# Attention and a gated MLP on one core: small tiles placed elsewhere in SBUF

## The chip, the cores and the metric

The kernel runs on one core of a Trainium2 chip. The metric is the device time of one launch in microseconds (us). The kernel before takes 735.44 us, the median of three runs (735.39 to 735.93). Its profile is of one further execution, which took 734.27 us and has a span of 732.5 us.

## The reference

Inputs are x (8 batches, 8 heads, 512 tokens, 64 wide) and state (the same with 32 tokens), float32. Cut to what matters:

```python
scores  = x @ state.T / 8 ;  a  = softmax(scores)  ; xread = a  @ state
scores2 = state @ x.T / 8 ;  a2 = softmax(scores2) ; sread = a2 @ x
y   = concat([xread, sread], axis=2)      # per batch 544 rows, heads joined to 512 columns
out = ((y @ w_a) * (y @ w_b)) @ w_out     # 512 -> 1536 -> 512
```

## The kernel before, in words

All heavy work is matrix products on TensorE. Each large product has 128 rows of contraction, 128 stationary columns (the weights) and 512 moving columns of 4 bytes, that is 2,048 bytes in each of the 128 SBUF partitions. Numbers are split into a high and a low part (type fp32r), so one product of the mathematics is three instructions: high by high, high by low, low by high.

The program has these kinds of product:

- **Layer 1** (output tile `ab`, function `layer1`): `(y @ w_a)` and `(y @ w_b)` for one of 12 strips of 128 hidden columns. Weights: slices of `p_h`, `p_l`. Moving: `at_h`, `at_l` (the attention weights of a batch; the state and the weights were multiplied beforehand into `p_h`, `p_l`). A strip is 2 x 2 x 3 = 12 instructions of 512 columns.
- **Layer 2** (output tile `acc`, function `layer2`): the gated strip times `w_out`. Weights: slices of `g_h`, `g_l`. Moving: the two halves of `wo0` ... `wo11`, of 2,048 bytes each. A strip is 4 blocks of tokens x 3 = 12 instructions of 512 columns.
- **Projections** (output tile `ms`, early `acc`, function `project`): the states times `w_a` and `w_b`. Weights: `sd_h`, `sd_l`. Moving: `wq`.
- **States** (output tile `ab`, class `States`): layer 1 for the rows of sread, 256 moving columns. Weights: `wq` and `sw_st`. Moving: `x_nat` and `x_raw`. Its layer 2 is as above.
- The attention's own products in full float32 (output `ms`), few and short.

ScalarE (ACT) and VectorE (DVE) move results out of PSUM, split them in two parts and convert the 64-bit weights; transfers are issued from SyncE (SP). The code records all instructions, and a planner (`plan`) then fixes one order for every engine from its own cost and due-time figures; all instructions of the program are issued from line 1047, which is why the profile's rows bear that line, and are told apart by their tiles.

**Where tiles stand in SBUF.** Pools are laid out one after the other in the order in which they are opened, each pool's tiles in turn, each with as many buffers as asked for. Below the first pool lie 16,512 bytes of each partition (32 x 512 + 128). Nearly all tiles have a multiple of 512 bytes a partition. Two do not: `m1` (3 x 16 numbers, 192 bytes, two buffers, 384 bytes in all) and `m2` (4 numbers, 8 buffers of 32 bytes, 256 bytes in all), both small tiles of the softmax in the pool `att`. So a tile's start past a multiple of 512 bytes depends on which of the two lie ahead of it. PSUM tiles are whole banks and are the same before and after.

Of the kernel before, what the change touches and what calls it, by code (L numbers as in the profile page):

```python
# [10 lines left out]
F32 = mybir.dt.float32  # L11
# [9 lines left out]
P = 128  # L21
# [393 lines left out]
def attn_moe(ctx, tc, xt, xn, sd, wl, w_out, out):  # L415
# [9 lines left out]
    def pool(name, bufs, free=False, **kw):  # L425
        p = Pool(ctx.enter_context(tc.tile_pool(name=name, bufs=bufs, **kw)), name, bufs, free)
        pools.append(p)
        return p

    const0 = ctx.enter_context(tc.tile_pool(name="const0", bufs=1))  # L430
    const = pool("const", 1)
    proj = pool("proj", 2)
    att = pool("att", 2)
    mlp = pool("mlp", 2)
    dram = pool("dram", 1, space=bass.MemoryType.DRAM)
    ps_acc = pool("ps_acc", 4, space=bass.MemoryType.PSUM)
# [6 lines left out]
    def minus(eng, out, in0, in1):  # L443
        eng.tensor_tensor(out=out, in0=in0, in1=in1, op=ALU.subtract)
# [149 lines left out]
    class Attention:  # L594
# [37 lines left out]

        def soft_t(self):

            m1 = self.m1 = att.tile([P, 3, 16], F32, name="m1")
            sp = self.sp
            t = self.t.rearrange("p (a b) -> p a b", b=32)
            nc.vector.tensor_reduce(out=m1[:, 0, :], in_=t, axis=AX.X, op=ALU.max)
            minus(nc.vector, sp, t, m1[:, 0, :].unsqueeze(2).broadcast_to([P, 16, 32]))
# [9 lines left out]

        def soft(self):  # L650

            m2 = self.m2 = att.tile([P, 4], F32, name="m2", bufs=8)
            nc.vector.tensor_reduce(out=m2[:, 0:1], in_=self.s, axis=AX.X, op=ALU.max)
            nc.vector.tensor_scalar_mul(out=m2[:, 1:2], in0=m2[:, 0:1], scalar1=-SCALE)
            if self.b not in WIDE:
                self.turn()
            nc.scalar.activation(out=self.e2, in_=self.s, func=AF.Exp, bias=m2[:, 1:2], scale=SCALE,
                                 accum_out=m2[:, 2:3])

        def turn(self):  # L660
            sp = self.sp
            nc.vector.transpose(out=sp.rearrange("p a b -> p (a b)"), in_=self.s)

            m1 = self.m1 = att.tile([P, 3, 16], F32, name="m1")
            nc.vector.tensor_reduce(out=m1[:, 0, :], in_=sp, axis=AX.X, op=ALU.max)
            minus(nc.vector, sp, sp, m1[:, 0, :].unsqueeze(2).broadcast_to([P, 16, 32]))

# [422 lines left out]
```

## Time and profile before

| | |
|---|---|
| median of 3 runs | 735.44 us |
| profiled execution | 734.27 us, span 732.5 us |
| TensorE (PE) busy | 706.2 us, 96% of the span, 3,440 matmuls |
| weight loads (PEld) busy | 557.7 us, beside the matmuls |
| VectorE (DVE) busy | 495.8 us, 68% |
| ScalarE (ACT) busy | 394.9 us, 54% |
| DMA | 134.32 MB, mean 183 GB/s |

Matmuls are pipelined: a row's duration (about 0.39 us for 512 columns) reaches into the next one. What a matmul costs when TensorE is full is the distance from its start to the start of the next, so the starts are what to read.

### The profile page before, as it was taken

Reading aid. Unit: us, or ns where it says so; the run is one execution under the profiler, and the core shown is the slowest. Engines: PE = TensorE matmul, PEld = TensorE weight load, DVE = VectorE, ACT = ScalarE, POOL = GpSimd, SP = SyncE. Lnnn points to the kernel's source line nnn. Section 1 sums busy time; section 2 is a strip of 40 time slices with the busy share of each in tenths; the row PEclk is TensorE's granted clock in tenths of the full one; section 3 lists DMA queues with packets and bytes.
Section 4 is the critical chain, followed back from the end, with each engine's and each line's share of the span. In section 5 each row is a group of like instructions: output and inputs, shape, how many; then the busy total and the mean of one; then the engine's idle time right before and its main releaser. Section 6 shows DMA issues by size and latency. Waiting matters only on the chain.

```text
span 732.5 us, 9629 instructions
## 1 busy us (share of the span) xinstructions
PE 706.2 (96%) x3440; PEld 557.7 (76%) x3440; DVE 495.8 (68%) x947; ACT 394.9 (54%) x723; POOL 0.7 (0%) x6
## 2 busy tenths in 40 slices
PE   5898899998999999999999999999999999999997
PEld 4565657785887888788888887886788888988886
DVE  5986795995847967684799548637879833795322
ACT  4966785686846459786445325234456433553222
POOL 0000000000000000000000000000000000000000
PEclk9999999999999999999999999999999999999999
DMA  9667867677788436859988133324425311501002
GB/s 339 219 225 276 278 238 241 240 278 268 259 286 309 158 142 243 272 193 354 356 314 288 38 115 123 115 64 134 159 57 198 119 58 30 199 31 30 1 0 87
DMA packets 55087, 134.32 MB, mean 183 GB/s; under 512 B 5632, under 2 KB 5632, under 8 KB 55040
## 3 DMA queue, kind: packets, MB, share of 16 engines
q1 hardware_dynamic: 55040, 133.71, 52.5%
q8 instruction: 27, 0.44, 0.3%
q14 instruction: 20, 0.16, 0.1%
HBM read 87.03 MB, written 46.66 MB: 183 GB/s over the span
## 4 chain that ended last, share of the span: by engine, by line
PE 92%; ACT 5%; DMA 1%; DVE 1%; issue 1%; DVEq 0%; SPq 0%; ACTq 0%
PE ab L1047 40%; PE acc L1047 39%; PE ms L1047 13%; ACT wq L1047 2%; DMA p_raw<-scr 1%; DMA x_raw<-xt 0%; ACT stg L1047 0%; ACT t L1047 0%; ACT wo L1047 0%; ACT p_h L1047 0%; ACT sd_h L1047 0%; ACT e L1047 0%; DVE m L1047 0%; ACT sw_st L1047 0%; ACT at_h L1047 0%
## 5 line engine op out<-in xcount | busy, mean ns | idle before, releaser
L1047 PE MATMUL acc<-wo,g_h 128*128 128x512 f32 x816 | 259.3, 397 | 0.1
L1047 PEld LDWEIGHTS acc<-wo,g_h 128*128 128x128 f32 x816 | 151.4, 188 | 37.0 <-issue 2.3
L1047 DVE TENSOR_TENSOR a_sb<-ab,a_sb 128x512 f32<-128x512 f32 (+1 forms) x108 | 71.3, 661 | 138.9 <-PE ab L1047 131.8
L1047 PE MATMUL acc<-wo,g_l 128*128 128x512 f32 x408 | 159.3, 396 | 0.0
L1047 PE MATMUL ab<-at_h,p_h 128*128 128x512 f32 x384 | 152.4, 400 | 1.9 <-ACT p_h L1047 1.7
L1047 PE MATMUL ab<-at_l,p_h 128*128 128x512 f32 x384 | 152.2, 397 | 0.0
L1047 PE MATMUL ab<-at_h,p_l 128*128 128x512 f32 x384 | 150.8, 396 | 0.0
L1047 ACT COPY a_sb<-ab 128x512 f32<-128x512 f32 (+1 forms) x108 | 60.9, 564 | 150.7 <-PE ab L1047 149.6
L1047 ACT CAST g_h<-a_sb 128x512 fp32r<-128x512 f32 (+1 forms) x108 | 64.6, 598 | 53.2 <-DVE a_sb L1047 52.9
L1047 PEld LDWEIGHTS acc<-wo,g_l 128*128 128x128 f32 x408 | 76.5, 188 | 18.3 <-issue 1.0
L1047 PEld LDWEIGHTS ab<-at_h,p_h 128*128 128x128 f32 x384 | 73.0, 190 | 22.4 <-ACT p_h L1047 3.6
L1047 PEld LDWEIGHTS ab<-at_h,p_l 128*128 128x128 f32 x384 | 72.7, 189 | 20.1 <-issue 3.1
L1047 PEld LDWEIGHTS ab<-at_l,p_h 128*128 128x128 f32 x384 | 72.9, 190 | 17.0 <-issue 1.8
L1047 DVE TENSOR_TENSOR g_l<-a_sb,g_h 128x512 fp32r<-128x512 f32 (+1 forms) x108 | 70.8, 655 | 20.9 <-ACT g_h L1047 20.8
L1047 DVE TENSOR_TENSOR p_l<-p_raw,p_h 128x512 fp32r<-128x512 f32 x92 | 60.0, 684 | 11.7 <-ACT p_h L1047 11.7
L1047 ACT CAST p_h<-p_raw 128x512 fp32r<-128x512 f32 x92 | 52.8, 619 | 13.8 <-PE ab L1047 9.3
L1047 DVE TENSOR_SCALAR t<-t 128x512 int32<-128x512 int32 x120 | 49.8, 422 | 9.6 <-ACT t L1047 8.5
L1047 PE MATMUL ms<-wq,sd_h 128*128 128x512 f32 (+2 forms) x112 | 38.8, 418 | 7.3 <-ACT wo L1047 3.9
L1047 ACT CAST wq<-t 64x512 fp32r<-64x512 f32 (+1 forms) x64 | 39.4, 619 | 8.2 <-PE ms L1047 2.9
L1047 DVE SCALAR_TENSOR_TENSOR t<-raw,t 128x512 int32<-128x512 int32 (+1 forms) x60 | 39.7, 686 | 0.3
L1047 PE MATMUL ms<-wq,sd_l 128*128 128x512 f32 (+2 forms) x112 | 37.7, 406 | 0.0
L1047 ACT COPY wo<-ms 128x512 f32<-128x512 f32 x44 | 25.8, 590 | 12.8 <-PE ms L1047 11.5
(93 smaller groups left out, 702.2 us busy)
## 6 DMA issues: line engine op xcount, KB each, us to landing
p_raw<-scr SPq DMA_DIRECT2D x46, 512.0 KB, 4.4
scr<-sw_st SPq DMA_DIRECT2D x48, 256.0 KB, 4.2
scr<-wo SPq DMA_DIRECT2D x48, 256.0 KB, 4.2
raw<-wl SPq DMA_DIRECT2D x22, 512.0 KB, 5.8
part<-stg SPq DMA_DIRECT2D x20, 512.0 KB, 3.0
stg<-part SPq DMA_DIRECT2D x20, 512.0 KB, 6.1
out<-stg SPq DMA_DIRECT2D x34, 256.0 KB, 2.4
x_raw<-xt SPq DMA_DIRECT2D x14, 576.0 KB, 3.9
```

What stands on the lines that cost most here:

```text
L1047: getattr(obj, method)(*map(real, args), **{k: real(x) for k, x in kw.items()})
```

## The change

The two small tiles get pools of their own: `m1` stands in a new pool `small`, opened ahead of all others, and `m2` in a new pool `tail`, opened behind `att`. Numbers of buffers (2 and 8) and shapes stay. No instruction, wait, transfer or order of an engine differs; only addresses do.

```diff
+    small = pool("small", 2)
     const0 = ctx.enter_context(tc.tile_pool(name="const0", bufs=1))
     const = pool("const", 1)
     proj = pool("proj", 2)
     att = pool("att", 2)
+    tail = pool("tail", 8)
     mlp = pool("mlp", 2)
...
-            m1 = self.m1 = att.tile([P, 3, 16], F32, name="m1")
+            m1 = self.m1 = small.tile([P, 3, 16], F32, name="m1")
...
-            m2 = self.m2 = att.tile([P, 4], F32, name="m2", bufs=8)
+            m2 = self.m2 = tail.tile([P, 4], F32, name="m2")
...
-            m1 = self.m1 = att.tile([P, 3, 16], F32, name="m1")
+            m1 = self.m1 = small.tile([P, 3, 16], F32, name="m1")
```

With `m1` ahead, everything from `ident` to `x_raw` moves up by 384 bytes. What stood between `m1` and `m2` stays, what stood between `m2` and the end of `att` moves down by 256, and the pool `mlp` stays. In bytes past a multiple of 512:

| tiles | before | after |
|---|---|---|
| `ident`, `xst`, `raw`, `t1`, `t2`, `wq`, `sd_h`, `sd_l`, `sw_st`, `wo0` to `wo11`, `x_raw` | 128 | 0 |
| `s_p`, `x_nat`, `at_h`, `at_l` | 0 | 0 |
| `e2`, `a2`, `a_tr` | 256 | 0 |
| `stg`, `p_raw`, `p_h`, `p_l`, `a_sb`, `g_h`, `g_l` | 256 | 256 |

As slices of tiles begin at multiples of 512 bytes, this is by kind of product:

| product | moving start before | after | weights' start before | after |
|---|---|---|---|---|
| layer 1 (`ab`, 512 columns) | 0 | 0 | 256 | 256 |
| layer 2 (`acc`) | 128 | 0 | 256 | 256 |
| projections (`ms<-wq,sd`) | 128 | 0 | 128 | 0 |
| states (`ab`, 256 columns) | 0 (`x_nat`), 128 (`x_raw`) | 0 | 128 | 0 |

## Rows read from the trace of the kernel before

**Rows 1.** The page: busy time by engine; chain that ended last, by engine and line
```profile
PE 706.2 (96%) x3440; PEld 557.7 (76%) x3440; DVE 495.8 (68%) x947; ACT 394.9 (54%) x723; POOL 0.7 (0%) x6
...
PE 92%; ACT 5%; DMA 1%; DVE 1%; issue 1%; DVEq 0%; SPq 0%; ACTq 0%
PE ab L1047 40%; PE acc L1047 39%; PE ms L1047 13%; ACT wq L1047 2%; DMA p_raw<-scr 1%; DMA x_raw<-xt 0%; ACT stg L1047 0%; ACT t L1047 0%; ACT wo L1047 0%; ACT p_h L1047 0%; ACT sd_h L1047 0%; ACT e L1047 0%; DVE m L1047 0%; ACT sw_st L1047 0%; ACT at_h L1047 0%
```
**Rows 2.** Windows: length, busy time by engine, granted clock, DMA share, GB/s
```profile
98.00:176.00 78.00, 77.86 (x368) 59.78 (x368) 63.66 (x124) 51.66 (x95) 0.00 (x0) 1.00 0.74 257
176.00:186.00 10.00, 6.44 (x19) 3.90 (x18) 6.44 (x12) 9.46 (x17) 0.00 (x0) 0.83 0.77 262
186.00:728.00 542.00, 542.00 (x2611) 438.36 (x2610) 349.58 (x655) 263.98 (x484) 0.00 (x0) 1.00 0.46 157
```
**Rows 3.** Matmuls by tiles, 98 to 728.2 us: count, busy, mean ns, idle before
```profile
L1047 PE MATMUL acc<-wo,g_h 128*128 128x512 f32 x778 | 246.9, 396 | 0.0
L1047 PE MATMUL acc<-wo,g_l 128*128 128x512 f32 x390 | 152.4, 396 | 0.0
L1047 PE MATMUL ab<-at_h,p_h 128*128 128x512 f32 x360 | 142.3, 397 | 0.6 <-ACT p_h L1047 0.4
...
L1047 PE MATMUL ms<-wq,sd_h 128*128 128x512 f32 (+1 forms) x86 | 32.2, 419 | 3.1 <-ACT wo L1047 2.4 <-ACT sw_st L1047 0.8
...
L1047 PE MATMUL ab<-x_nat,wq 128*128 128x256 f32 x128 | 24.2, 281 | 0.0
```
**Rows 4.** The chain that ended last, pieces in time: start, length, what
```profile
349.13 2.73 PE ab L1047 x12
351.86 2.79 PE acc L1047 x12
354.66 2.73 PE ab L1047 x12
...
434.76 2.79 PE acc L1047 x12
```
**Rows 5.** Timeline of TensorE, 404 to 410 us: start, duration, instructions
```profile
404.23 0.39 PE L1047 MATMUL ab<-at_h,p_h 128*128 128x512 f32 x1
...
404.93 0.39 PE L1047 MATMUL ab<-at_h,p_h 128*128 128x512 f32 x1
...
406.97 0.62 PE L1047 MATMUL acc<-wo,g_h 128*128 128x512 f32 x2
...
409.76 0.39 PE L1047 MATMUL ab<-at_h,p_h 128*128 128x512 f32 x1
```
**Rows 6.** Timeline of all engines, end of the span, from 725.3 us
```profile
725.34 0.42 DVE L1047 TENSOR_TENSOR g_l<-a_sb,g_h 128x256 fp32r<-128x256 f32 x1 [0.47 <-ACT g_h L1047]
725.57 1.08 PE L1047 MATMUL acc<-wo,g_h 128*128 128x512 f32 x4
...
727.89 0.62 PE L1047 MATMUL acc<-wo,g_l 128*128 128x512 f32 x2
728.32 1.29 DVE L1047 TENSOR_TENSOR stg<-acc,stg 128x512 f32<-128x512 f32 x2 [2.55 <-PE acc L1047]
```
**Rows 7.** Timeline of TensorE: two projections, and a run of state products
```profile
101.37 0.39 PE L1047 MATMUL ms<-wq,sd_h 128*128 128x512 f32 x1
...
101.83 0.39 PE L1047 MATMUL ab<-at_l,p_h 128*128 128x512 f32 x1
...
720.66 0.28 PE L1047 MATMUL ab<-x_nat,sw_st 128*128 128x256 f32 x1
...
722.89 0.39 PE L1047 MATMUL acc<-wo,g_h 128*128 128x512 f32 x1
```
**Rows 8.** Timeline of TensorE around the one long stall behind 98 us
```profile
178.54 0.40 PE L1047 MATMUL ms<-wq,sd_l 128*128 128x512 f32 x1
181.30 0.50 PE L1047 MATMUL ms<-wq,sd_h 128*128 128x512 f32 x1 [2.36 <-ACT wo L1047]
...
183.96 0.63 PE L1047 MATMUL ab<-at_h,p_h 128*128 128x512 f32 x1
...
185.24 0.63 PE L1047 MATMUL ab<-at_h,p_h 128*128 128x512 f32 x1
```
**Rows 9.** Costliest groups by form: VectorE, tiles at 256, 128 and 0 bytes
```profile
L1047 DVE TENSOR_TENSOR g_l<-a_sb,g_h 128x512 fp32r<-128x512 f32 x96 | 65.7, 685 | 18.8 <-ACT g_h L1047 18.8
...
L1047 DVE SCALAR_TENSOR_TENSOR t<-raw,t 128x512 int32<-128x512 int32 x30 | 20.6, 686 | 0.2
...
L1047 DVE TENSOR_TENSOR s_p<-s_p,m 128x512 f32<-128x512 f32 x28 | 19.3, 690 | 0.8
```

## The prediction

> **What bounds the kernel now.** I read the page first, then windows, the chain of waits, and last the starts of single matmuls. The page's busy line and its chain [rows 1] show TensorE busy for 96% of the span and on the chain for 92% of it, layer 1 (`ab`) and layer 2 (`acc`) with 40% and 39%. The windows [rows 2] tell where that holds: from 98 to 176 us TensorE is busy for 77.86 of 78 us, from 186 to 728 us for all of 542 us, and only 176 to 186 us has a hole. In that whole stretch its idle time before matmuls of these kinds is 3.1 + 0.6 us, all of it behind ScalarE, none behind a transfer or VectorE [rows 3]. So behind 98 us a nanosecond saved per matmul is a nanosecond saved per matmul of the span; ahead of 98 us TensorE waits for others in many places, and I count nothing there.
>
> A busy TensorE is not one at its peak, so the next view is the chain in order of time [rows 4]. Between 349 and 437 us it is nothing but strips of 12 layer 1 matmuls and 12 layer 2 matmuls in turn. Both strips stream 12 x 512 columns with 12 weight loads, and yet layer 1 takes 2.73 us and layer 2 takes 2.79 us, each time. From the start at 351.86 to that at 434.76 there are 15 pairs: 82.90 / 15 = 5.527 us a pair.
>
> The timeline resolves this [rows 5]. Layer 2 goes from 406.97 to 409.76: 2.79 / 12 = 232.5 ns from start to start. Layer 1 has two speeds: its first three matmuls behind layer 2 go from 404.23 to 404.93, 0.70 / 3 = 233 ns, and the other nine from 404.93 to 406.97, 2.04 / 9 = 226.7 ns. [...]
>
> Is it other engines that disturb layer 2? At the end of the span no: VectorE's last work before the final results ends at 725.76 (725.34 + 0.42), and TensorE alone then takes 727.89 - 725.57 = 2.32 us for 10 layer 2 matmuls, the same 232 ns [rows 6].
>
> **The change part by part.** No instruction is added, removed or moved. What differs between layers 1 and 2 in the supply of operands is in the table of starts: the weights of both stand 256 bytes past a multiple of 512, the moving operand of layer 1 on the multiple, that of layer 2 128 bytes past it. A run of 2,048 bytes touches four pieces of 512 bytes from a multiple, and five from 128 past it. The change gives layer 2 the pair of starts that layer 1 has.
>
> *Layer 2.* 778 + 390 = 1,168 matmuls stand behind 98 us [rows 3]. If layer 2 runs as layer 1 does with its slow first three (2.735 us a strip, between the 2.73 of [rows 4] and the 2.74 of [rows 5]), each saves (2.79 - 2.735) / 12 = 4.6 ns: 5.4 us. If it runs as the nine do, 232.5 - 226.7 = 5.8 ns: 6.8 us. Bound on the other side: it stays, 0 us, or gets worse by as much as it could gain, -6.8 us, since no row shows this operand at another start. I take 5.4 us, the nearest row being layer 1's whole strip.
>
> *Layer 1.* Its first three matmuls behind layer 2 are slow with starts that are as good as those of the other nine, so they pay for what went before them. With layer 2 no longer different the cause would go: 0.70 - 3 x 0.2267 = 0.02 us by the rows; by the pair of 5.527 us, less 24 x 0.2267 = 5.440, less layer 2's 12 x 5.8 ns = 0.070, it is 0.017 us. Of 3 x 360 = 1,080 layer 1 matmuls behind 98 us [rows 3] make 90 strips: 1.5 us. Bounds 0 and 1.5; I take all of it, because the two layers then have equal starts.
>
> *Projections.* 2 x 86 = 172 matmuls. They now run at (101.83 - 101.37) / 2 = 230 ns [rows 7] with both operands 128 past; afterwards both are on the multiple, a pair that no row shows. Between the 226.7 ns of the best row and a loss as large, 3.3 ns x 172 = 0.6 us either way. I take 0.
>
> *States.* 128 + 64 + 64 + 32 = 288 matmuls of 256 columns, of which [rows 3] shows the first group. They take (722.89 - 720.66) / 19 = 117 ns [rows 7] with a moving start now of 0, now of 128, and weights at 128; afterwards 0 and 0. [...] I take 0.
>
> *VectorE, ScalarE, transfers.* The same kind of VectorE operation takes 685 ns with operands at 256, 690 at 0 and 686 at 128 [rows 9]: no effect of the start. Transfers to moved tiles may land sooner or later; TensorE waits for none behind 98 us [rows 3], so work of TensorE covers them. If that cover went, a late one would show as a new wait.
>
> *Who is late next.* In the hole at 176 to 186 us ScalarE is busy for 9.46 of 10 us [rows 2]; the stall of 2.36 us [rows 8] is ScalarE's. Its work there starts from a projection's result, so TensorE's gain ahead of it should pass on. If it does not, what layer 2 won before 176 us is lost: by the windows' counts (368 of 368 + 19 + 2,611 matmuls) 143 of the 1,168, x 4.6 ns, about 0.7 us. The lower clock behind the hole costs about 7 matmuls x 200 ns = 1.4 us (427 against 227); a shorter or longer hole could move this. I leave both in the range.
>
> Sum: 5.4 + 1.5 = 6.9 us off the profiled execution's 734.27 us, of which 732.5 are span. Its time lies 1.2 us below the median of 735.44, which I take as the base: 735.44 - 6.9 = 728.5 us.
>
> [...]
>
> **The rivals.**
> *The start is not what tells the layers apart.* Layer 2 also changes its moving half at each instruction and uses four PSUM banks in turn, where layer 1 stays in one for six matmuls. Then nothing changes: 735.4 us. For it: it needs no effect of addresses, which VectorE does not have either [rows 9]. Against: layer 1 changes its moving operand as well (`at_h`, `at_l`), and the slow three of layer 1 fall in the same bank as three fast ones [rows 5].
> [...]
> *Gains that do not pass on.* Layer 2 gets faster and ScalarE's hole, or VectorE elsewhere, takes back some: with half of 6.9 us kept, 732.0 us. Against: no idle time of TensorE from 186 to 728 us [rows 2].
>
> **How the numbers follow.** The forecast (728.5 us) 0.70; gains half kept (732.0) 0.11; nothing changes (735.4) 0.11; reads that meet (741.4) 0.08. A difference under 0.2%, about 1.5 us, can hardly be told from none with this kernel. The forecast's own range reaches from all gains together (6.8 + 1.5 + 0.6 + 1.0 = 9.9 us, 725.5) to layer 2 alone without the part before 176 us (5.4 - 0.7 = 4.7, 730.7). For 8 in 10 the range is taken up to the case without change: 725.5 to 735.5 us. Faster 0.81, same 0.11, slower 0.08.
>
> **What would show it.** Layer 2's strips in the chain at 2.73 us or below instead of 2.79 confirm the main term; layer 1's first three at 227 ns, and pairs of 5.44 to 5.47 us, the second. Strips that stay at 2.79 make it wrong, and point to the first rival. [...] A hole at 176 us that grows by what was won shows the third. VectorE's 685 to 690 ns should stay.

## The result, and the profile after

The changed kernel takes 727.55 us (median of 6 runs, 726.73 to 729.3), the kernel before beside it 735.54 us (6 runs, 735.27 to 739.15). The ratio is 0.9886, 95% interval 0.9864 to 0.9907: 8.0 us faster, where 6.9 were forecast. The profiled execution took 727.69 us with a span of 725.9 us, 6.6 us below the profiled one of before.

The page of the changed kernel, busy time, against [rows 1]:

```profile
PE 699.4 (96%) x3440; PEld 559.2 (77%) x3440; DVE 495.3 (68%) x947; ACT 395.1 (54%) x723; POOL 0.7 (0%) x6
```

Only TensorE's busy time moved, by 6.8 us; VectorE, ScalarE and the weight loads stayed within 1.5 us. The chain of waits in order of time, against [rows 4] (start, length, what):

```profile
346.67 2.72 PE ab L1049 x12
349.39 2.72 PE acc L1049 x12
...
430.99 2.72 PE acc L1049 x12
```

The two layers now take the same. From 349.39 to 430.99 there are 15 pairs: 81.60 / 15 = 5.440 us, where before it was 5.527. The timeline of TensorE, against [rows 5] (start, duration, instruction):

```profile
400.91 0.39 PE L1049 MATMUL ab<-at_h,p_h 128*128 128x512 f32 x1
...
401.59 0.39 PE L1049 MATMUL ab<-at_h,p_h 128*128 128x512 f32 x1
...
403.63 0.62 PE L1049 MATMUL acc<-wo,g_h 128*128 128x512 f32 x2
...
406.35 0.39 PE L1049 MATMUL ab<-at_h,p_h 128*128 128x512 f32 x1
```

Layer 1's first three behind layer 2 take 0.68 / 3, its other nine 2.04 / 9 and layer 2 2.72 / 12: 227 ns, 226.7 and 226.7. The slow three are gone. The windows, against [rows 2] (length, busy time by engine, granted clock, DMA share, GB/s):

```profile
176.00:186.00 10.00, 7.13 (x18) 5.02 (x17) 7.14 (x14) 9.73 (x18) 0.00 (x0) 0.66 0.88 293
186.00:722.00 536.00, 535.25 (x2609) 438.43 (x2607) 348.23 (x653) 262.77 (x482) 0.00 (x0) 1.00 0.46 158
```

The granted clock around the hole is 0.66 instead of 0.83. Behind it TensorE is almost as full as before, but not quite: it is idle for 0.75 us from 186 us on, where before it was for none.

**Where the lead grows.** The same instruction starts in both traces, so the distance of its two starts shows how far the changed kernel is ahead there. Landmarks of the changed kernel on TensorE's timeline:

```profile
101.10 0.39 PE L1049 MATMUL ms<-wq,sd_h 128*128 128x512 f32 x1
...
177.15 0.40 PE L1049 MATMUL ms<-wq,sd_l 128*128 128x512 f32 x1
179.91 0.80 PE L1049 MATMUL ms<-wq,sd_h 128*128 128x512 f32 x1 [2.37 <-ACT wo L1049]
180.51 0.63 PE L1049 MATMUL ms<-wq,sd_l 128*128 128x512 f32 x1
...
185.63 0.61 PE L1049 MATMUL ab<-at_h,p_h 128*128 128x512 f32 x1
...
186.54 0.40 PE L1049 MATMUL ms<-wq,sd_h 128*128 128x512 f32 x1
...
625.46 0.63 PE L1049 MATMUL acc<-wo,g_h 128*128 128x512 f32 x2
...
628.21 0.28 PE L1049 MATMUL ab<-x_nat,wq 128*128 128x256 f32 x1
...
721.32 0.61 PE L1049 MATMUL acc<-wo,g_l 128*128 128x512 f32 x2
```

and those of the kernel before that stand in no group above:

```profile
182.12 0.39 PE L1047 MATMUL ms<-wq,sd_l 128*128 128x512 f32 x1
182.94 0.79 PE L1047 MATMUL ab<-at_h,p_h 128*128 128x512 f32 x1 [0.43 <-ACT p_h L1047]
...
187.21 0.39 PE L1047 MATMUL ms<-wq,sd_h 128*128 128x512 f32 x1
...
315.51 0.72 PE L1047 MATMUL acc<-wo,g_h 128*128 128x512 f32 x2
...
631.13 0.62 PE L1047 MATMUL acc<-wo,g_h 128*128 128x512 f32 x2
...
633.92 0.28 PE L1047 MATMUL ab<-x_nat,wq 128*128 128x256 f32 x1
```

With [rows 4, 6 to 8] the lead is 0.27 us at the first landmark (101.37 - 101.10), 1.39 at the stall (178.54 - 177.15), 0.67 behind it (187.21 - 186.54), 2.47 and 3.77 at the two ends of the run of pairs (351.86 - 349.39, 434.76 - 430.99), and 6.57 at the last layer 2 (727.89 - 721.32). Four things follow.

- In plain strips it grows by (3.77 - 2.47) / 15 = 0.087 us a pair, which is 12 x 5.8 ns of layer 2 and 0.017 of layer 1.
- The stall is as long as before: 2.76 us from start to start in both (179.91 - 177.15; 181.30 - 178.54). But behind it 12 matmuls take (185.63 - 180.51) / 12 = 427 ns and a 13th as much, at a granted clock of 0.50 (0.50 from 180.6 to 185.6 us). Before, the first three behind the stall took 0.82 us together (182.12 - 181.30), 273 ns each; TensorE then waited a second time, behind `p_h` (182.94), and only there 6 matmuls ran at that level (granted clock 0.50 from 183 to 186 us), up to the return of the full clock at 186.06 (1.00 from 186.1 to 190 us). That is 7 x 200 ns = 1.4 us more. The slower matmuls now cover the second wait; so 1.39 - 0.67 = 0.72 us is what is lost in all, in these two executions.
- TensorE has two waits behind ScalarE that the kernel before does not have:

```profile
305.82 0.51 PE L1049 MATMUL ab<-at_h,p_h 128*128 128x512 f32 x1 [0.44 <-ACT p_h L1049]
...
313.70 0.73 PE L1049 MATMUL acc<-wo,g_h 128*128 128x512 f32 x2 [0.24 <-ACT g_h L1049]
```

The lead falls there from 2.78 us, at a projection just ahead of them (307.43 - 304.65), to 1.81 (315.51 - 313.70).
- Where states alternate with layer 2 it doesn't grow at all. ScalarE's copies out of layer 1's result mark this, in the kernel before and in the changed one:

```profile
624.34 0.37 ACT L1047 COPY a_sb<-ab 128x256 f32<-128x256 f32 x1 [2.84 <-PE ab L1047]
...
648.13 0.59 ACT L1047 COPY a_sb<-ab 128x512 f32<-128x512 f32 x1 [1.40 <-PE ab L1047]
```

```profile
618.65 0.37 ACT L1049 COPY a_sb<-ab 128x256 f32<-128x256 f32 x1 [2.77 <-PE ab L1049]
...
642.42 0.59 ACT L1049 COPY a_sb<-ab 128x512 f32<-128x512 f32 x1 [1.36 <-PE ab L1049]
```

The lead is 5.69 at the first and 5.71 at the second, 24 us later. A strip of layer 2 there went from 2.79 (633.92 - 631.13) to 2.75 us (628.21 - 625.46), and the states gave that back.

### The profile page after: what moved, and what is told of

Read it like the earlier page. It is cut to its first block, busy times and chain, and to the rows that moved or that the text cites. A ratio compares the mean times of both kernels' runs of the same rounds, so it can differ in the third digit from the quotient of the medians.

```text
span 725.9 us, 9629 instructions
## 1 busy us (share of the span) xinstructions
PE 699.4 (96%) x3440; PEld 559.2 (77%) x3440; DVE 495.3 (68%) x947; ACT 395.1 (54%) x723; POOL 0.7 (0%) x6
## 4 chain that ended last, share of the span: by engine, by line
PE 89%; DVE 4%; ACT 4%; DMA 2%; issue 1%; DVEq 0%; SPq 0%; ACTq 0%
PE ab L1049 39%; PE acc L1049 37%; PE ms L1049 12%; DMA raw<-wl 2%; DVE t L1049 2%; ACT wq L1049 2%; DVE m L1049 1%; DMA x_raw<-xt 0%; ACT wo L1049 0%; DVE s_p L1049 0%; ACT t L1049 0%; DVE wq L1049 0%; DVE p_l L1049 0%; ACT sd_h L1049 0%; DVE raw L1049 0%
## 5 line engine op out<-in xcount | busy, mean ns | idle before, releaser
L1049 PE MATMUL acc<-wo,g_h 128*128 128x512 f32 x816 | 255.9, 393 | 0.4 <-ACT g_h L1049 0.2
L1049 PE MATMUL acc<-wo,g_l 128*128 128x512 f32 x408 | 157.4, 392 | 0.0
```

Of the source, the lines that this page charges most:

```text
L1049: getattr(obj, method)(*map(real, args), **{k: real(x) for k, x in kw.items()})
```

## The experiments

The theory to begin with was the prediction's: the moving operand should start on a multiple of 512 bytes. Its main rival was that the distance of the moving operand's start from that of the weights counts, and beside them stood a theory in which starts on multiples of 256 are enough.

**1. A map by itself.** A kernel of nothing but streams of 24 matmuls of type fp32r, with weights and moving operand at chosen starts past a multiple of 512 (second argument of `W` and `M`); it leaves the whole computation out.

```diff
+    N = 24
+    for i in range(N): mm(bb[:, :512], lhsT=W(i, 256), rhs=M(i, 4, 512), start=(i == 0), stop=(i == N - 1))
+    for i in range(N): mm(aa[:, :512], lhsT=W(i, 256), rhs=M(i, 16, 512), start=(i == 0), stop=(i == N - 1))
...
```

> This kernel leaves out the whole computation. It runs streams of 24 matmuls each, weights reloaded for every one, on TensorE alone: 512, 384, 256 and 128 columns of fp32r, some of bf16, with the moving operand and the weights started at chosen bytes past a multiple of 512. What is read is the distance from start to start in each stream. Theory A (only the moving start counts, and it is best on a multiple of 512): every 512-column stream with the moving start on 0 takes 226.7 ns whatever the weights' start, one with 128 takes 232 to 233 ns whatever the weights' start, and the starts between 0 and 512 lie between 227 and 238. Theory B (the distance of the two starts counts, 256 is best): moving 128 with weights 384 takes 226.7 ns, moving 0 with weights 0 takes 230 ns or more. [...] Theory D (the start matters only to multiples of 256): 0 and 256 take 226.7 ns, 128 and 384 take 232.

Its chain (start, length of a stream, line). Moving and weights start at 0 and 256 in L53, 4 and 256 in L54, 128 and 256 in L59, 0 and 0 in L66, 0 and 128 in L68, 128 and 128 in L75; L97 has 64 and 256 in bf16:

```profile
25.71 5.44 PE aa L53 x24
31.16 5.68 PE bb L54 x24
...
59.08 5.60 PE aa L59 x24
...
98.06 5.46 PE bb L66 x24
...
109.12 5.58 PE bb L68 x24
...
147.95 5.46 PE aa L75 x24
...
245.66 5.18 PE aa L97 x24
```

With the moving operand at 0 a stream is fast (L53, 226.7 ns) or slow (L68, 232.5 ns), by where the weights start; at 128 it is slow (L59) and fast (L75). So the moving operand's start alone decides nothing. What orders all streams is the distance of the two starts modulo 256 bytes: 0 is fast, 128 and 192 cost 5 to 7 ns a matmul, 64 about 2, and 4 the most (L54, 236.7 ns). Two streams at a distance of 256, L80 and L83, take 5.49 us; by the starts in the trace they lose it in their first eight or nine matmuls and then run at 226.7 ns too, which experiment 10 comes back to. The forecast's theory falls, and starts that are multiples of 16 bytes do not all take the same time either (L53 5.44, L59 5.60 us); the rival holds, but with 0 as good as 256. In bf16 all streams take 5.18 / 24 = 215.8 ns.

**2. All operands at 128.** Each of the two buffers of `m1` is made 64 bytes longer, so everything behind it, weights and moving operands alike, goes up by another 128 bytes: 128 and 384 for the two layers, 128 and 128 for projections and states.

```diff
-            m1 = self.m1 = small.tile([P, 3, 16], F32, name="m1")
+            m1 = self.m1 = small.tile([P, 4, 16], F32, name="m1")
```

> The changed kernel with the small tile ahead made 128 bytes longer, so that every operand stands 128 bytes further on: moving operands of both layers at 128 past a multiple of 512, weights of both at 384; projections and states have both at 128. Distances between moving operand and weights are those of the changed kernel. Theory A (the moving start counts): layer 1 and layer 2 both at 232.5 ns, 1,168 + 1,080 + 172 matmuls x 5.8 ns = 14.0 us over the changed kernel, about 741.5 us, strips of 2.79 us in both layers. Theory B (the distance counts): the changed kernel's 727.5 us, strips of 2.72 us.

727.96 us (4 runs), ratio 0.990 [0.987, 0.993]. Its chain:

```profile
350.48 2.72 PE acc L1049 x12
353.19 2.72 PE ab L1049 x12
```

Every moving operand stands 128 past a multiple of 512, and both layers stay at 2.72 us. This is the run that sinks the prediction's mechanism in the kernel itself, and with it the theory that asks for multiples of 256.

**3. Layer 1 at 256 and 256, layer 2 at 0 and 256.**

```diff
-    att = pool("att", 2)
     tail = pool("tail", 8)
+    att = pool("att", 2)
```

> The changed kernel with the second small pool (256 bytes) opened ahead of the pool of attention tiles in place of behind it: layer 1's moving operand goes to 256 past a multiple of 512, with its weights at 256; layer 2 keeps moving 0 and weights 256. Theory A (the moving start counts, on multiples of 512): layer 1 slows to about layer 2's old speed, 1,080 x 5.8 ns = 6.3 us, and some more for layer 2's first three of each strip: 733.8 to 735.5 us. Theory D (multiples of 256 are enough): 727.5 us. Theory B (the distance counts, here 0 for layer 1): layer 1 at 230 ns or more, 731 us or more, and layer 2 unchanged.

728.68 us (4 runs), ratio 0.9903 [0.987, 0.9936], strips of 2.72 us: as the changed kernel. The moving start of 256 does no harm, and neither does a distance of 0 instead of 256. The distance modulo 256 gives this; so would starts on multiples of 256, but for experiment 2.

**4. `m1` moved, `m2` left where it was.**

```diff
-            m2 = self.m2 = tail.tile([P, 4], F32, name="m2")
+            m2 = self.m2 = att.tile([P, 4], F32, name="m2", bufs=8)
```

> One part of the change alone: the tile of 192 bytes goes ahead of all others, the other small tile stays in the pool of attention tiles. Only the three attention tiles behind it keep their 256 bytes past a multiple of 512. All theories: as the changed kernel within 0.3 us, 727.5 us, since no large product reads those tiles.

728.13 us (4 runs), ratio 0.9906 [0.9873, 0.9939]. The second edit of the change does nothing that these runs can tell.

**5. The map, finer.** Streams of 36 with the weights at 0.

> This kernel leaves out the whole computation: streams of 36 matmuls on TensorE alone, weights reloaded for each, weights at 0 and the moving start at 0 to 256 past a multiple of 512 in steps of 16; then weights of 128, 64 and 32 columns at distance 0 and 128; streams whose weights alternate between distance 0 and 128; 256 columns at eight distances; plain float32 at distance 0 and 128. Theory B2 (what counts is the distance of the moving start from the weights' start, modulo 256 bytes, because the two reads of SBUF run side by side): for 512 columns 226.7 ns at 0 and 256, 229 at 64, 232 to 234 at 128 and 192; with 64 and 32 weight columns, whose read is short, the difference between distances 0 and 128 shrinks to a half and a quarter of 6 ns; alternating streams lie between, 228 to 234; 256 columns: 120 ns at 0, 118.4 at 128. Theory A2 (the weights play no part): the difference between 0 and 128 stays whatever the weights' columns. Theory E (the fp32r format's own): plain float32 shows no difference.

Its chain. Distances: L71 0, L54 8, L58 64, L62 128, L69 240, L70 256; in L78 the weights change at each matmul, so that the distance is 0 and 128 in turn; L87 has 256 columns at 192; L89 and L90 are plain float32 at 0 and 128 (two passes each, hence 72):

```profile
38.69 8.41 PE bb L54 x36
...
72.23 8.24 PE bb L58 x36
...
105.53 8.36 PE bb L62 x36
...
164.35 8.16 PE aa L69 x36
172.51 8.20 PE bb L70 x36
180.71 8.16 PE aa L71 x36
...
238.59 8.35 PE bb L78 x36
...
289.10 4.11 PE aa L87 x36
297.47 30.90 PE aa L89 x72
328.37 30.91 PE bb L90 x72
```

8.16 us are 226.7 ns a matmul; 8 bytes of distance (233.6 ns) cost no less than 128 (232.2), 64 costs 2 ns, and 240 nothing. The stream whose distance changes from 0 to 128 and back takes 231.9 ns and not the mean of the two, 229.5: it is about as slow as the one at 128 throughout. Float32 takes 429 ns a pass at either distance. With weights of 64 or 32 columns the difference between 0 and 128 is gone (8.27 and 8.26 us for 64, 8.33 and 8.30 for 32), but because distance 0 gets slower too: the expected halving and quartering did not come. What in the reading of weights and columns makes this pattern stays open.

**6. Only the weights moved.** The pool `mlp` goes up by 128 bytes; all moving operands of the two layers stay on multiples of 512.

```diff
-            tt = att.tile([P, S], F32, name="a_tr", bufs=1)
+            tt = att.tile([P, S + 32], F32, name="a_tr", bufs=1)[:, :S]
```

> The changed kernel with one attention tile of the pool ahead of the last large pool made 128 bytes longer, so that only that pool moves: the weights of both layers go from 256 to 384 past a multiple of 512. Moving operands stay on multiples of 512; projections and states stay as in the changed kernel. Theory A (the moving start counts): as the changed kernel, 727.5 us. Theory B2 (the distance counts modulo 256; here 128 for both layers): both layers at 232.0 to 233.5 ns as in the streams, strips of 2.79 us, (1,168 + 1,080) x 5.6 to 6.6 ns = 12.6 to 14.8 us over the changed kernel, 740 to 742.5 us, slower than the kernel before by 5 to 7 us.

739.48 us (10 runs), ratio 1.0056 [1.0039, 1.0073]: slower than before, and 11.6 us above the changed kernel run beside it (8). Its chain:

```profile
352.88 2.79 PE acc L1049 x12
355.68 2.79 PE ab L1049 x12
```

With their moving operands where the forecast wanted them, both layers now run as layer 2 did before.

**7. The same at a distance of 64** (`S + 48` in place of `S + 32`).

> The same with 192 bytes in place of 128: weights of both layers at 448, moving operands on multiples of 512, a distance of 64 modulo 256. Theory B2: 228.7 ns in both layers, 2,248 x 2.1 ns = 4.7 us over the changed kernel, 732.2 us, strips of 2.745 us. Theory A: 727.5 us. A theory in which any distance but 0 costs the same: 740 us or more.

732.42 us (7 runs), ratio 0.9975 [0.9935, 1.0015], strips of 2.75 us: between the changed kernel (727.92) and the one before (735.43), by the 2 ns a matmul that the map has at 64. One of the seven runs took 741.9 us and widens the interval, so that by the times alone it can't be told from the kernel before; the strips tell it.

**8 and 9. The changed kernel again**, beside the runs of the second and the third round.

> The changed kernel itself, for a comparison on the same chip as its variants: 727.5 us, strips of 2.72 us.

> The changed kernel again, beside the three variants that follow: 727.5 to 728 us; 13 to 14 matmuls of 427 ns behind the stall at 177 us.

727.92 us, 0.9899 [0.9871, 0.9928], and 728.24 us, 0.9905 [0.9891, 0.9919] (4 runs each). The hole is not the same each time. In the profiled execution of 8, 12 matmuls take 427 ns behind the stall. In that of 9 (729.6 us) it is not the 13 to 14 that were expected: two do, then TensorE waits for `p_h` as in the kernel before (1.61 us from start to start, 182.99 to 184.60), and behind that seven more do.

**10. States at a distance of 192**, the best that the map has for 256 columns, with 0 for every other product: layer 1 at 64 and 64, layer 2 at 128 and 128.

```diff
+    gate = pool("gate", LAG + 1)
+    small = pool("small", 2)
     att = pool("att", 2)
-    tail = pool("tail", 8)
     mlp = pool("mlp", 2)
+    tail = pool("tail", 8)
...
-            m1 = self.m1 = small.tile([P, 3, 16], F32, name="m1")
+            m1 = self.m1 = small.tile([P, 56], F32, name="m1")[:, :48].rearrange("p (a b) -> p a b", b=16)
...
-        gh = mlp.tile([P, 512], F32R, name="g_h", bufs=LAG + 1)[:, :u.n]
+        gh = gate.tile([P, 512], F32R, name="g_h")[:, :u.n]
```

> Pools laid out so that the two layers and the projections keep a distance of 0 modulo 256 between moving operand and weights, and the states' products get 192 in place of 0: the two gate tiles get a pool of their own behind the converted weights, the first small tile (rows of 224 bytes) stands between that and the attention tiles, the second at the very end. No instruction or order differs. Theory B2 (the distance counts, and for 256 columns 192 is best): states' products at 113.3 ns where they stand in a row, in place of 119.5, less where they follow others: 288 x 3 to 6 ns = 0.9 to 1.8 us under the changed kernel, 726 to 727 us; layers stay at 226.7 ns. Theory A2 (the weights play no part): no difference.

731.18 us (7 runs), ratio 0.9951 [0.9932, 0.997]: 3 us worse than the changed kernel, a miss. Its timeline of TensorE:

```profile
352.51 0.39 PE L1050 MATMUL ab<-at_h,p_h 128*128 128x512 f32 x1
...
353.20 0.39 PE L1050 MATMUL ab<-at_h,p_h 128*128 128x512 f32 x1
...
355.24 0.62 PE L1050 MATMUL acc<-wo,g_h 128*128 128x512 f32 x2
...
358.00 0.39 PE L1050 MATMUL ab<-at_h,p_h 128*128 128x512 f32 x1
```

In both layers the two starts have distance 0, and yet strips that follow one another are slower than 2.72: layer 1 takes 2.73 us (355.24 - 352.51), layer 2 2.76 (358.00 - 355.24), 0.05 us a pair. Layer 1 loses it in its first three matmuls, 0.69 / 3 = 230 ns, and its other nine take 2.04 / 9 = 226.7. The states take 117.7 ns here, not the 4.11 / 36 = 114 of the isolated stream. So a product can be slow for some matmuls behind one with other starts, as layer 1's slow three were in the kernel before. The second map has such a switch by itself: L69 and L70 differ in the moving start alone (240 and 256), and each comes to 226.7 ns, but L70 needs 8.20 us, and L71, whose starts are L70's modulo 256, 8.16. By the starts in the trace it is L70's first eight matmuls that are slow. That only the matmul at the switch meets the other product's operands would not explain eight. Nor are unequal starts all of it: in the changed kernel a strip of layer 2 behind states takes 2.75 us too, with all starts equal modulo 256. What is carried over from one product to the next stays open.

**11 and 12. Projections spread.** Four projections that stood together ahead of the hole go between blocks of layer 2; 12 adds this to 10. The question is whether the hole falls apart, and with it the stretch behind it in which 13 matmuls took 427 ns each. The line that changes TensorE's order `pe` (`acc` are nine matmuls of layer 2, which stood first, `proj` four projections of two):

```diff
+    pe[a:b] = [proj[0]] + acc[:3] + [proj[1]] + acc[3:6] + [proj[2]] + acc[6:] + [proj[3]]
```

> The changed kernel with another order on TensorE alone in one place: four projections that stand behind a strip of layer 2, and behind which TensorE waits for ScalarE at 175 to 180 us, go between the strip's blocks of three. [...] Theory G (the hole is ScalarE's work alone, and the clock behind it costs nothing in the end): 727.5 us.

> Both edits together, the layout with the states at a distance of 192 and the spread projections. If both gains stand, they add up: 722 to 726 us; otherwise the larger of the two.

728.46 us (4 runs), 0.9907 [0.9894, 0.992], and 730.63 us (5 runs), 0.9936 [0.9924, 0.9949]: nothing gained over the kernels without it that is clear of the noise, where 12 was to take 722 to 726 us if both gains stood. TensorE's timeline of run 11:

```profile
179.15 0.50 PE L1092 MATMUL ms<-wq,sd_h 128*128 128x512 f32 x1 [2.14 <-ACT wo L1092]
...
182.22 0.80 PE L1092 MATMUL ab<-at_h,p_h 128*128 128x512 f32 x1 [1.85 <-ACT p_h L1092]
```

The one wait of 2.37 us became two of 2.14 and 1.85 us, both ScalarE's, and the lower clock still came behind the second: 11 matmuls took (187.50 - 182.81) / 11 = 426 ns each. What that clock costs by itself stays open. No kernel tried is faster than the changed one.

## Why the prediction was right, and where it was wrong

**Time.** 727.55 us against 728.5, inside the range; direction and place of the gain were right, and so was the reading that TensorE is full. That the size came so near is in part luck. Between matmuls that follow one another without a wait in both traces, the starts from 98 us on sum up to 5.8 us won in layer 2 (5.4 in the forecast), 1.9 in layer 1 (1.5), 0.6 in the projections (0) and 0.4 lost in the states (0): 7.9 us. The waits and the lower clock took back 1.6 of it, which the sum had at nothing; with 0.3 us won ahead of 98 us that leaves the 6.6 us between the two profiled executions. The medians are 8.0 us apart, as the profiled execution of before lay below its median.

**Layer 2.** The size per matmul was taken from layer 1's whole strip, 4.6 ns; plain strips gained 5.8, the other bound. Counting it for all 1,168 was too much on the other hand: where states alternate with layer 2 a strip gained 0.04 us instead of 0.07, and that went to the states.

**Layer 1's slow three.** 0.70 to 0.68 us, as forecast.

**Projections and states, taken at 0.** Projections won 0.6 us, as much as their bound, and states lost 0.4. No run shows the 1.0 us that the forecast's range counts for the states; what the runs show is those 0.4 us. The 19 states of [rows 7] now go from 714.11 to 716.38, 119.5 ns against 117. The forecast's 230 ns for a projection came from two steps alone: four that stand in a row go from 175.63 to 176.31 in the kernel before and from 174.24 to 174.92 in the changed one, 0.68 / 3 = 227 ns in both.

**The hole, and gains that do not pass on.** The wait itself did not grow, so the mark of *gains that do not pass on* did not show. The lower clock lasted for 13 matmuls of 427 ns and not 6, which with the wait that it covered cost 0.72 us; the forecast had left this in the range without a direction. But part of what this rival says came about elsewhere: at 305 and 313 us TensorE, now earlier, waits for ScalarE, and the lead falls by 1.0 us. The forecast had no such wait, because [rows 2] showed no idle time behind 186 us.

**VectorE** keeps 685, 686 and 690 ns for the forms of [rows 9].

**The step that failed** is the cause: "A run of 2,048 bytes touches four pieces of 512 bytes from a multiple, and five from 128 past it." Experiment 2 has five pieces everywhere and keeps the gain, experiment 6 has four and loses it. What counts in these runs is the distance of the two starts modulo 256 (226.7 ns a matmul at 0, 232.2 at 128). That the direction came out right all the same is luck as far as the cause goes: the change brings the moving operand of layer 2 to the multiple and so also to a distance of 256 from its weights; the table of starts before held one slow case, at both a start and a distance of 128, and could not tell the two apart. The sentence "the change gives layer 2 the pair of starts that layer 1 has" was enough for the sum.

**The rivals.** That the start is not what tells the layers apart is excluded by 6, in which nothing but addresses differs. *Reads that meet*, equal starts as the worst distance, had the right kind of cause with the wrong sign: at a distance of 0 a matmul took 226.7 ns, at 128 232.2. No run shows the losses of projections and states from which its 741.4 us was added up; in the changed kernel a projection took 227 ns and a state 119.5. The sign was in the trace: projections, with equal starts, ran at 230 ns by the forecast's row and at 227 in a longer run, which the forecast did not turn into a theory of its own.

## What to carry to other kernels

Where a full TensorE streams 512 columns of fp32r, give the weights and the moving operands of all products that alternate the same start modulo 256 bytes (here 226.7 ns a matmul, against 232.2 at a distance of 128); small tiles of odd size belong in a pool where they shift none of these. Read it from start to start in the timeline, since the durations of overlapped matmuls (0.39 us in both kernels) hide it. A case in which two explanations share all their points calls for one kernel in which they part, here one operand moved alone, before the cause is written down.

## What the hardware showed unexpectedly

- A distance of 8 bytes costs as much as one of 128 (234 and 232 ns, against 226.7), one of 4 bytes more (237 ns), and 240 costs nothing: not an alignment in the usual sense. Of the three types tried fp32r alone showed an effect: bf16 took 215.8 ns at 0, 16, 32, 64 and 128, plain float32 429 ns a pass at 0 and 128. These two were not tried at 4, 8 and 240.
- In streams of 256 columns the best distance is another one: 114 ns at 192 (4.11 / 36), 120 at 0. The kernel of experiment 10 could not get it.
- Behind a wait of the same length, 2.76 us from start to start, the clock differed between these executions. In the kernel before it fell (granted 0.50, 427 ns a matmul) only behind the next wait, for 6 matmuls; in the changed kernel at once, for 12 or 13, or for 2 and then 7 behind the next wait.
- Behind a switch to other starts some products of fp32r ran slower at first: L70 of the second map in eight matmuls (8.20 us in all, against L71's 8.16), and layer 1 of the kernel before in three, at 233 ns against 226.7 in the other nine.
